# Projections as pairs of 64-row matmuls with max-pass tiles between them, and a written issue order on every engine

## The chip, the core and the metric

The kernel runs on one core of one Trainium2 chip. The metric is the device time of one execution in microseconds. A core has a matrix engine (TensorE, PE in the profile, its weight loads PEld), a vector engine (VectorE, DVE), an activation engine (ScalarE, ACT), a general engine (GpSimd, POOL) and a queue engine that only issues transfers (SyncE, SP).

## The reference

The result mixes two blocks over the same x (2048 tokens, 640 channels) with a gate per token.

```python
x = A_x
g = sigmoid((x * gate_w).sum(-1, keepdims=True))
# A: attention, 32 heads of 20 channels
q, k, v = split(x @ wqkv)
p = softmax(einsum("bhqd,bhkd->bhqk", q, k) * 20 ** -0.5)
a = merge(einsum("bhqk,bhkd->bhqd", p, v)) @ wo
# B: MLP over the token axis
h = layernorm(x, axis=-1, eps=1e-5)
u = gelu(einsum("bsd,sf->bdf", h, w1) + b1)      # f = 1728
b = transpose(einsum("bdf,fs->bds", u, w2) + b2)
return g * a + (1 - g) * b
```

## The kernel before

All matmuls are done on numbers split into a high part in a rounded float32 format and a low part, the rest. A product of two such numbers is three passes: high by high, high by low, low by high (`mm3`, L48). The split is `hi_lo` (L36): ACT copies to the high part, and DVE or POOL subtracts it from the source.

The kernel runs in stages that follow each other on PE.

1. Projections. q and k first: `qk_unit(m, w, q)` (L213) computes 128 channels (m = 0 to 4 are q, 5 to 9 are k) for a quarter q of the tokens, 512 columns. It is 15 full 128-row matmuls into one PSUM bank (five chunks of the 640 input channels by three passes). ACT copies the bank to the high part `evh`, DVE subtracts to the low part `evl`, and SP stores both to DRAM (`q_d`, `k_d`, L223). The units of m = 0 and 5 come first, interleaved, while `load_x` (L229) brings x in by quarters (five loads `xr` of 256 KB each, split into `xh` and `xl`). Then eight units of m = 1 and 6, then 32 v units (L293; 128 tokens by half of the heads, 322 or 320 columns, 15 matmuls each), then the 24 q/k units of the other m. The first v half also yields the sum for the gate and the mean of each token (`gs`); `stats_unit` (L289) runs a Square with accumulation on ACT for the variance. After the v units, `rstd`, `g_t`, `omg` and `b2o` (L319 to L325) are made by a chain that goes back and forth between ACT and DVE. Beside the last 24 units the first half of x is normalised (`h_norm`, POOL) and split (`h_split`, ACT and POOL).
2. The MLP (`mlp`, L489). Its matmuls are pairs of 64-row matmuls into two banks (`pair64`, L43): each uses one half of PE's rows, and the two sums are added when they are read.
3. The attention loop (L672): 16 pairs of heads, 32 iterations each. An iteration makes four score tiles `st` (62 rows by 512 columns), ACT takes their exp into `p`, and PE multiplies `p` by v.
4. The last product with `wo`, and the mix.

The exp needs the maximum of each row of scores beforehand. That is the max pass: a stream of 2048 tiles `s` (60 rows by 512 columns, `s_tiles`, L168), each a matmul and a DVE reduction (`mx`, L180), in pairs of tiles that use the two halves of PE's rows. `s_next` (L155) issues one tile. Each pair of heads p needs a stack in SBUF of its q and k (`load_stack`, 18 loads of 80 and 160 KB, through `base_stack` or, in the loop, `s_stack`). 736 tiles are spread over the MLP (`S_AHEAD`, L538), the other 1312 over the loop. How many an iteration takes is a counter:

```python
due = min((p * 32 + it + 1) * LEFT // (NP * 32 - 28) + 1, LEFT)
take = min(due - given, 3)
```

The PSUM banks are eight: four for `st` (shared with the projections and the MLP), three for `s`, one for the sum of p by v. Tiles with the same tag reuse their buffers in turn, and an instruction waits until the buffer it writes is free.

The order of PE's instructions is written by hand throughout (L32). ACT and DVE join at L236, before the first unit. POOL and SP join only at L328, after the v units; before that a scheduler orders what they issue. The first score stack is issued by POOL (`base_stack(0, False, nc.gpsimd)`, beside the 18th of the last 24 units).

Of the kernel before, what the change touches and what calls it, by code (L numbers as in the profile page):

```python
# [13 lines left out]
P = 128  # L14
S, D, H, DH, F = 2048, 640, 32, 20, 1728
NP = H // 2
NT = S // P
# [11 lines left out]
def gated_mix(ctx, tc, xT, x, wqk, wv0, wv1, wo, w1, w1t, b1, w2, b2, out):  # L29
# [51 lines left out]
    nc.gpsimd.memset(ones_s, 1.0)  # L81
    ones = dram.tile([2, S], F32, name="ones_d")
    nc.gpsimd.dma_start(ones, ones_s)
    eps_t = cp.tile([P, 1], F32, name="eps_t")
# [32 lines left out]
    def base_stack(p, full, eng=nc.sync):  # L117
        ks = k8([P, S], F32R, f"ks{p}_{full}")
        qs = [q4([P, S // 2], F32R, f"qs{p}_{full}_{i}") for i in range(2)]
        load_stack(p, ks, qs, full, eng)  # L120
        return ks, qs
# [74 lines left out]
    xl = [[p1.tile([P, 512], F32R, name=f"xl{c}_{q}") for q in range(4)] for c in range(NC)]  # L196

    def w_dma(m):
# [4 lines left out]
    def load_w(m, raw=None):  # L203
        if raw is None:
            raw = w_dma(m)
        wh = q4([P, NC, P], F32R, f"wh{m}")
        wl = q4([P, NC, P], F32R, f"wl{m}")
        hi_lo(wh, wl, raw, hi_eng=nc.scalar)
        return wh, wl

    accs = iter(range(1000))

    def qk_unit(m, w, q):  # L213
        wh, wl = w
        ps = st_tile([P, 512], f"qk{m}_{q}")
        mm3(ps, [(wh[:, c], wl[:, c], xh[c][q], xl[c][q]) for c in range(NC)])
        hi = p1.tile([P, 512], F32R, tag="evh", bufs=2, name=f"evh{m}_{q}")
        lo = p1.tile([P, 512], F32R, tag="evl", bufs=2, name=f"evl{m}_{q}")
        hi_lo(hi, lo, ps, hi_eng=nc.scalar)
        dst = q_d if m < NC else k_d  # L220
        rows = slice((m % NC) * P, (m % NC + 1) * P)
        cols = slice(q * 512, (q + 1) * 512)
        nc.sync.dma_start(dst[0, rows, cols], hi.bitcast(F32))  # L223
        nc.sync.dma_start(dst[1, rows, cols], lo.bitcast(F32))

# [16 lines left out]
    raws = [w_dma(0), w_dma(NC)]  # L242
    w = {0: load_w(0, raws[0])}
    load_x(0)
    w[NC] = load_w(NC, raws[1])
    for q in range(4):
        if q < 3:
            load_x(q + 1)
        if q == 2:
            w[1] = load_w(1)  # L250
        qk_unit(0, w[0], q)
        qk_unit(NC, w[NC], q)
    pxs.close()
# [14 lines left out]
    def split_wv(half, c):  # L268
        hi_lo(wvs[half][0][c], wvs[half][1][c], wv_raw.pop((half, c)), hi_eng=nc.scalar)

    for c in range(NC):
        load_wv(0, c)
    for n in range(8):
        qk_unit((1, NC + 1)[n // 4], w[(1, NC + 1)[n // 4]], n % 4)
        if n == 0:
            w[NC + 1] = load_w(NC + 1)
        if n >= 3:
            split_wv(0, n - 3)
            load_wv(1, n - 3)
    nc.gpsimd.dma_start(b1_t, b1)  # L280
    nc.gpsimd.dma_start(b2_t, b2)
# [10 lines left out]

    for half in range(2):  # L293
        wvh, wvl = wvs[half]
        width = HALF + 2 if half == 0 else HALF
        for t in range(NT):
# [4 lines left out]
            if n == NT:  # L301
                nc.vector.tensor_scalar_mul(negm, gs[:, :, 1], -1.0 / D)
            if n in (2, 4, 6, 8, 10):
                split_wv(1, n // 2 - 1)
            if n == 2 * NT - 4:
                w[2] = load_w(2)
            ps = st_tile([P, width], f"v{half}_{t}")
            q, cols = t // 4, slice((t % 4) * P, (t % 4 + 1) * P)
            mm3(ps, [(xh[c][q][:, cols], xl[c][q][:, cols], wvh[c], wvl[c]) for c in range(NC)])
            vt = pvp.tile([P, 16, VW], F32, tag="vt", bufs=3, name=f"vt{half}_{t}")  # L310
            nc.gpsimd.memset(vt[:, :, DH], 1.0)
            nc.scalar.activation(vt[:, :, :DH], ps[:, :HALF].rearrange("p (h w) -> p h w", w=DH), AF.Copy)
            nc.sync.dma_start(v_d[half, t], vt.rearrange("p h w -> p (h w)"))
            if half == 0:
                nc.vector.tensor_copy(gs[:, t], ps[:, HALF:])
            else:
                stats_unit(t)
                stats_load(t + 4)
    nc.scalar.activation(rstd, ssq, AF.Sqrt, bias=eps_t, scale=1.0 / D)  # L319
# [4 lines left out]
    nc.vector.tensor_scalar(omg, g_t, -1.0, 1.0, op0=OP.mult, op1=OP.add)  # L324
    nc.vector.tensor_mul(b2o, b2_t, omg)  # L325
    pvs.close()

    ordered.enter_context(tc.manual_schedule(engines={EG.Pool, EG.SP}))  # L328
    hps = ExitStack()
# [33 lines left out]
    AHEAD = 4  # L363
    w_tmp = [k8([P, 16, P], F32R, f"wtmp{i}") for i in range(2)]
    w_raws, w_got = [], []
# [11 lines left out]
    def w_split(k):  # L377
        src, tail = w_list[k]
        raw = w_raws[k]
        n, m = src.shape[1], src.shape[2]  # L380
        if k < AHEAD:
            o = 8 * (k % 2)
            hi, lo = w_tmp[k // 2][:, o: o + 4], w_tmp[k // 2][:, o + 4: o + 8]
# [18 lines left out]
    for n, (m, q) in enumerate(units):  # L402
        if q == 0 and n + 4 < len(units):
            w[units[n + 4][0]] = load_w(units[n + 4][0])
# [8 lines left out]
        if n == 17:  # L413
            w_raw(0)
            w_raw(1)
        qk_unit(m, w[m], q)
        if n in (18, 19):
            w_split(n - 18)
        if n in (20, 21):
            w_raw(n - 18)  # L420
        if n in (22, 23):
            w_split(n - 20)
    p1s.close()

    gps = ExitStack()
    gp = gps.enter_context(tc.tile_pool(name="gp", bufs=1, side="right"))

    soon = []

    def settle(all_=False):  # L430
        for e in soon:
            e[0] -= 1
        due = [e for e in soon if all_ or e[0] <= 0]
        for e in due:
            soon.remove(e)
            e[1]()

# [99 lines left out]

    S_AHEAD = 736  # L538
    STEPS = 2 * ((FT - 1) * 48 + 32 + NT * 40)

    def start_ahead(p):
        if 2 <= p + 1 < 6:
            s_src[p + 1] = base_stack(p + 1, False, None)

    hooks[0] = start_ahead
    steps = mlp(hs)
    done = 0
    for n, _ in enumerate(steps):
        settle()
        while done + 2 <= S_AHEAD and done < S_AHEAD * (n + 1) / STEPS:  # L550
            if done == 48:
                s_src[1] = base_stack(1, False, None)
            if done == 4 * 128 + 40:
# [4 lines left out]
            if drip and done % 4 == 0:  # L558
                drip.pop(0)()
# [26 lines left out]
    M_LAG[0] = 0  # L586
    s_src[6] = s_stack(6)

# [83 lines left out]
    for p in range(NP):  # L672
# [3 lines left out]
        for it in range(32):  # L676
            qh, kt = divmod(it, NT)
            if p + 1 < NP:
                if it == 6:
                    st_src[p + 1] = base_stack(p + 1, True)  # L680
                if it == 12:
                    load_v(p + 1)
                if it == 27:
                    load_m(p + 1, st_src[p + 1][1], 0)
            if it == 11 and p:
                load_m(p, qs, 1)
            if it == 14 and due_stack:
                n = due_stack.pop()
# [109 lines left out]
```

## Time and profile before

| | |
|---|---|
| median of 3 runs | 1846.74 us |
| lowest and highest | 1844.78 and 1847.63 us |
| the profiled execution | 1846.6 us |
| its span, first to last instruction | 1844.8 us |
| granted clock of TensorE over the span | 0.996 |
| q/k units of m = 0, 5, 1, 6 | 7.0 to 65.0 us of the span |
| v units | 65.0 to 136.4 |
| q/k units of the other m | 136.4 to 225.3 |
| MLP | 225.3 to 698.0 |
| attention loop | 698 to 1763 |
| last product and mix | 1763 to 1845 |

The times of the stages are read from the matmuls of PE in the trace, as microseconds from the first instruction. The profiled execution has 1.8 us around its span.

### The profile page before, as it was taken

What the parts mean: (1) busy time and instruction counts of PE and PEld (TensorE: products, weight loads), DVE (VectorE), ACT (ScalarE), POOL (GpSimd) and SP (SyncE); (2) the same over time, 40 slices, a digit from 0 to 9 for tenths busy, and PEclk for the clock granted to TensorE, in tenths of its full rate; (3) what the DMA queues carried; (4) which work ended last, traced back from release to release, by engine and by line L of the source; (5) the groups of instructions that cost most, each with busy time, mean ns of one, the idle gap of its engine ahead of it and who ended that gap; (6) DMA issues with size and microseconds to landing.
All of it is one profiled execution on the core that took longest, in us unless ns stands there. A gap on an engine that the chain in (4) does not pass through costs nothing. (4 is left out here: it accounts for less than half of the span.)

```text
span 1844.8 us, 39129 instructions
## 1 busy us (share of the span) xinstructions
PE 1829.7 (99%) x14978; PEld 1135.2 (62%) x14978; DVE 1428.9 (77%) x2341; ACT 1361.6 (74%) x2688; POOL 637.1 (35%) x900
## 2 busy tenths in 40 slices
PE   9999999999999999999999999999999999999998
PEld 7998799999999994333333333333333333333378
DVE  4202299999999998888888888888888888888137
ACT  4243244465444448999999999999999999999930
POOL 1013478888887770112112111121321211212210
PEclk9999999999999999999999999999999999999999
DMA  8456766566645645504032324213540423301463
GB/s 289 143 169 212 222 173 173 158 194 193 168 139 166 189 136 121 118 15 103 20 85 61 73 42 93 57 50 78 107 103 24 109 47 77 71 14 23 131 219 132
DMA packets 152831, 216.61 MB, mean 117 GB/s; under 512 B 65698, under 2 KB 92082, under 8 KB 148738
## 3 DMA queue, kind: packets, MB, share of 16 engines
q1 hardware_dynamic: 129172, 178.68, 35.4%
q0 software_dynamic: 14688, 20.78, 5.2%
q10 hardware_dynamic: 8784, 14.65, 2.4%
q8 instruction: 118, 1.93, 0.4%
q14 instruction: 69, 0.57, 0.1%
HBM read 165.43 MB, written 48.25 MB: 116 GB/s over the span
## 5 line engine op out<-in xcount | busy, mean ns | idle before, releaser
L180 DVE TENSOR_REDUCE mx<-s 128x1 f32<-128x512 f32 x2048 | 1293.7, 684 | 159.9 <-PE s L178 119.7
L703 ACT ACTIVATE p<-st 128x512 f32<-128x512 f32 x2048 | 1042.1, 615 | 20.9 <-PE s L178 2.2
L700 PEld LDWEIGHTS st<-qs_True,ks_True 62*128 62x128 f32 x2048 | 307.3, 185 | 485.1 <-ACT p L703 312.9
L700 PE MATMUL st<-qs_True,ks_True 62*128 62x512 f32 x2048 | 579.6, 425 | 0.2 <-ACT ty L477 0.2
L637 PE MATMUL pv<-p,v 128*32 128x512 f32 x4096 | 555.5, 605 | 0.2
L178 PE MATMUL s<-sk,sq 60*128 60x512 f32 x1280 | 423.1, 434 | 0.0
L41 POOL TENSOR_TENSOR wl<-wr,wh 128x512 fp32r<-128x512 f32 x228 | 273.6, 1216 | 59.8 <-ACT wh L38 30.9
L624 POOL DMA_DIRECT2D o_d<-oev x128 | 67.0, 524 | 494.3 <-DVE oev L618 491.6
L178 PE MATMUL s<-ks_False,qs_False 60*128 60x512 f32 x768 | 225.1, 397 | 0.4 <-DVE mx L180 0.3
L46 PE MATMUL y<-gh,wh 64*128 64x320 f32 x896 | 216.8, 308 | 0.0
L46 PE MATMUL y<-gl,wh 64*128 64x320 f32 x832 | 210.3, 306 | 0.0
L46 PE MATMUL y<-gh,wl 64*128 64x320 f32 x832 | 209.4, 305 | 0.0
L38 ACT ACTIVATE wh<-wr 128x512 fp32r<-128x512 f32 (+2 forms) x246 | 135.9, 594 | 90.2 <-PE s L178 29.0
L178 PEld LDWEIGHTS s<-sk,sq 60*128 60x128 f32 x1280 | 197.7, 185 | 1.2
L637 PEld LDWEIGHTS pv<-p,v 128*32 128x32 f32 x4096 | 84.9, 108 | 171.4 <-issue 156.4
L46 PE MATMUL u<-hl,wh 64*128 64x320 f32 x864 | 167.1, 306 | 0.0
L46 PE MATMUL u<-hh,wh 64*128 64x320 f32 x864 | 167.1, 306 | 0.0
L46 PE MATMUL u<-hh,wl 64*128 64x320 f32 x800 | 156.9, 306 | 0.4 <-POOL wl L41 0.4
L46 PEld LDWEIGHTS y<-gh,wh 64*128 64x128 f32 x896 | 155.3, 184 | 0.4
L46 PEld LDWEIGHTS y<-gh,wl 64*128 64x128 f32 x832 | 147.0, 184 | 0.3
L46 PEld LDWEIGHTS y<-gl,wh 64*128 64x128 f32 x832 | 146.9, 184 | 0.0
L178 PEld LDWEIGHTS s<-ks_False,qs_False 60*128 60x128 f32 x768 | 124.4, 184 | 1.1 <-DVE mx L180 1.1
(124 smaller groups left out, 1817.6 us busy)
## 6 DMA issues: line engine op xcount, KB each, us to landing
wr<-in_w_dram SPq DMA_DIRECT2D x196, 256.0 KB
ks_True<-k_d SPq DMA_DIRECT2D x96, 160.0 KB
qs_True<-q_d SPq DMA_DIRECT2D x192, 80.0 KB
sk<-k_d SPq DMA_DIRECT2D x60, 160.0 KB
sq<-q_d SPq DMA_DIRECT2D x120, 80.0 KB
v_d<-vt SPq DMA_DIRECT2D x32, 168.0 KB
v<-v_d SPq DMA_DIRECT2D x16, 336.0 KB
xr<-in_xT_dram SPq DMA_DIRECT2D x20, 256.0 KB
```

The lines of the kernel that those rows point to most:

```text
L38: nc.scalar.activation(hi, src, AF.Copy)
L41: (lo_eng or nc.vector).tensor_sub(lo, src, hi.bitcast(F32))
L46: nc.tensor.matmul(ps[k], a[r], b[r], start=start, stop=stop)
L178: nc.tensor.matmul(ps, qs[half][r, t * P:(t + 1) * P], ks[r, kc * 512:(kc + 1) * 512], start=True, stop=True)
L180: nc.vector.tensor_reduce(mx[:, kc, j, t: t + 1], ps, axis=AX.X, op=OP.max)
L624: nc.gpsimd.dma_start(o_d[DH * h: DH * h + DH, cols], ev[r: r + DH, :])
L637: nc.tensor.matmul(pv[r: r + 32, :], v_tiles[p][:, kt, 10 * j: 10 * j + 32], pts[j, c], start=(kt == 0), stop=(kt == NT - 1))
L700: nc.tensor.matmul(ps, ks[r, kt * P:(kt + 1) * P], qs[qh][r, c * 512:(c + 1) * 512], start=True, stop=True)
L703: nc.scalar.activation(pt, ps, AF.Exp, scale=SCALE)
```

## The change

The projections go over to pairs of 64-row matmuls in two banks (`mm_pairs` calls `pair64`). A unit is now read in three steps: ACT copies the first bank at the unit's end, DVE adds the second bank to it three or four PE steps later, and (for q and k) ACT and POOL split it six steps later; SP stores it after twelve. These steps stand in a list `soon`, which `settle` works off at each step of the next unit. v's units are done alike, without the split.

Between the pairs, 176 tiles of the max pass are issued (`Q_S`): four per q/k unit from the fifth unit of m = 1 and 6 on, two per v unit. The MLP keeps its 736 tiles, so 1136 are left to the loop. The score stacks of the first two pairs of heads are loaded in between, one transfer at every second step, by SP. POOL and SP issue in the written order from the start. Subtractions of weights and of q and k go from DVE to POOL; the loads for the statistics go from POOL to SP, and their Square runs two units later. Stacks of the attention loop are asked for at iteration 18 and 23 instead of 6 and 14.

```diff
-        return base.tile(shape, dt, tag="q4", bufs=6, name=name)
+        return base.tile(shape, dt, tag="q4", bufs=4, name=name)
+    Q_S, V_RATE, EVL = 176, 2, 3
...
+    def run(gen, rate):
+        nonlocal done, credit
+        for n, _ in enumerate(gen):
+            settle()
+            if drip and n % 2:
+                drip.pop(0)()
+            credit += rate
+            while credit >= 2 and done < Q_S:
+                credit -= 2
+                s_next()
+                s_next()
+                done += 2
+
+    def mm_pairs(ps, ops):
+        for n, (ah, al, bh, bl) in enumerate(ops):
+            for i, (a, b) in enumerate(((ah, bh), (ah, bl), (al, bh))):
+                pair64(ps, a, b, n == i == 0, n == len(ops) - 1 and i == 2)
+                yield
+
     def qk_unit(m, w, q):
-        ps = st_tile([P, 512], f"qk{m}_{q}")
-        mm3(ps, [(wh[:, c], wl[:, c], xh[c][q], xl[c][q]) for c in range(NC)])
+        ps = [st_tile([P, 512], f"qk{m}_{q}_{i}") for i in range(2)]
+        yield from mm_pairs(ps, [(wh[:, c], wl[:, c], xh[c][q], xl[c][q]) for c in range(NC)])
...
-        hi_lo(hi, lo, ps, hi_eng=nc.scalar)
+        full = lo.bitcast(F32)
+        nc.scalar.activation(full, ps[0], AF.Copy)
+
+        def split():
+            nc.scalar.activation(hi, full, AF.Copy)
+            nc.gpsimd.tensor_sub(lo, full, hi.bitcast(F32))
...
+        soon.append([3, lambda: nc.vector.tensor_add(full, ps[1], full)])
+        soon.append([6, split])
+        soon.append([12, store])
...
-    ordered.enter_context(tc.manual_schedule(engines={EG.Activation, EG.DVE}))
+    ordered.enter_context(tc.manual_schedule(engines={EG.Activation, EG.DVE, EG.Pool, EG.SP}))
...
+        if n == 1:
+            w[NC + 1] = load_w(NC + 1, raws[0])
+            ks = k8([P, S], F32R, "ks0")
+            qq = k8([P, S], F32R, "qs0")
+            s_src[0] = (ks, [qq[:, :S // 2], qq[:, S // 2:]])
+            load_stack(0, *s_src[0], False, None)
+        if n == 4:
+            s_src[1] = base_stack(1, False, None)
+        run(qk_unit((1, NC + 1)[n // 4], w[(1, NC + 1)[n // 4]], n % 4), 4 / 15 if n >= 4 else 0)
...
-            nc.gpsimd.dma_start(xjs[t], x[t * P:(t + 1) * P, :])
+            nc.sync.dma_start(xjs[t], x[t * P:(t + 1) * P, :])
...
+            run(v_unit(half, t), V_RATE / 15)
+            if half and t >= 2:
+                stats_unit(t - 2)
+                stats_load(t + 2)
+    for t in range(NT - 2, NT):
+        stats_unit(t)
     nc.scalar.activation(rstd, ssq, AF.Sqrt, bias=eps_t, scale=1.0 / D)
...
     nc.vector.tensor_mul(b2o, b2_t, omg)
+    settle(True)
     pvs.close()
-    ordered.enter_context(tc.manual_schedule(engines={EG.Pool, EG.SP}))
...
-        if n == 17:
-            s_src[0] = base_stack(0, False, nc.gpsimd)
...
-        qk_unit(m, w[m], q)
+        run(qk_unit(m, w[m], q), 4 / 15)
...
-    S_AHEAD = 736
+    S_AHEAD = Q_S + 736
...
-                if it == 6:
+                if it == 18:
                     st_src[p + 1] = base_stack(p + 1, True)
-                if it == 12:
+                if it == 21:
                     load_v(p + 1)
...
-            if it == 14 and due_stack:
+            if it == 23 and due_stack:
```

More of the change, by code (lines that the diff above doesn't have):

```diff
@@ L118, in base_stack @@
         ks = k8([P, S], F32R, f"ks{p}_{full}")
-        qs = [q4([P, S // 2], F32R, f"qs{p}_{full}_{i}") for i in range(2)]
+        if p % 3 == 1 and not full:
+            qs = [base.tile([P, S // 2], F32R, tag="q4b", bufs=2, name=f"qs{p}_{i}") for i in range(2)]
+        else:
+            qs = [q4([P, S // 2], F32R, f"qs{p}_{full}_{i}") for i in range(2)]
         load_stack(p, ks, qs, full, eng)
@@ L196, in gated_mix, with settle @@
     xl = [[p1.tile([P, 512], F32R, name=f"xl{c}_{q}") for q in range(4)] for c in range(NC)]
+    soon = []
+    def settle(all_=False):
+        for e in soon:
+            e[0] -= 1
+        due = [e for e in soon if all_ or e[0] <= 0]
+        for e in due:
+            soon.remove(e)
+            e[1]()
     def w_dma(m):
@@ L220, in qk_unit @@
[L220 to L224, printed above, removed]
+        lo = p1.tile([P, 512], F32R, tag="evl", bufs=EVL, name=f"evl{m}_{q}")
+        full = lo.bitcast(F32)
[3 more added lines that the diff above has]
+            nc.gpsimd.tensor_sub(lo, full, hi.bitcast(F32))
@@ L226, in gated_mix, with store @@
+        def store():
+            dst = q_d if m < NC else k_d
+            rows = slice((m % NC) * P, (m % NC + 1) * P)
+            cols = slice(q * 512, (q + 1) * 512)
+            nc.sync.dma_start(dst[0, rows, cols], hi.bitcast(F32))
+            nc.sync.dma_start(dst[1, rows, cols], lo.bitcast(F32))
+        soon.append([3, lambda: nc.vector.tensor_add(full, ps[1], full)])
+        soon.append([6, split])
+        soon.append([12, store])
     pxs = ExitStack()
@@ L249, in gated_mix @@
         if q == 2:
[L250 to L252 removed]
+            raws = [w_dma(1)]
+        if q == 3:
+            w[1] = load_w(1, raws[0])
+        run(qk_unit(0, w[0], q), 0)
+        run(qk_unit(NC, w[NC], q), 0)
     pxs.close()
@@ L305, in gated_mix @@
             if n == 2 * NT - 4:
[L306 to L318, printed above, removed]
+                raws = [w_dma(2)]
+            if n == 2 * NT - 2:
+                w[2] = load_w(2, raws[0])
+            run(v_unit(half, t), V_RATE / 15)
[4 more added lines that the diff above has]
+        stats_unit(t)
     nc.scalar.activation(rstd, ssq, AF.Sqrt, bias=eps_t, scale=1.0 / D)
@@ L363, in gated_mix @@
     AHEAD = 4
-    w_tmp = [k8([P, 16, P], F32R, f"wtmp{i}") for i in range(2)]
+    w_tmp = k8([P, 16, P], F32R, "wtmp")
     w_raws, w_got = [], []
@@ L403, in gated_mix @@
         if q == 0 and n + 4 < len(units):
-            w[units[n + 4][0]] = load_w(units[n + 4][0])
-        if n == 17:
-            s_src[0] = base_stack(0, False, nc.gpsimd)
+            raws = [w_dma(units[n + 4][0])]
+        if q == 1 and n + 3 < len(units):
+            w[units[n + 3][0]] = load_w(units[n + 3][0], raws[0])
         if 3 <= n < NT + 3:
@@ L422, in gated_mix @@
             w_split(n - 20)
+    settle(True)
+    while done < Q_S:
+        s_next()
+        done += 1
     p1s.close()
@@ L546, in gated_mix @@
     steps = mlp(hs)
-    done = 0
+    s_src[2] = base_stack(2, False, None)
     for n, _ in enumerate(steps):
         settle()
[L550 to L553, printed above, removed]
+        while done + 2 <= S_AHEAD and done < Q_S + (S_AHEAD - Q_S) * (n + 1) / STEPS:
+            if done == 6 * 128 + 40:
                 st_src[0] = base_stack(0, True, None)
@@ L557, in gated_mix @@
                 drip.append(lambda: load_v(0))
-            if drip and done % 4 == 0:
+            if drip:
                 drip.pop(0)()
```

77 lines of the change are left out of this document (43 added, 34 removed).

## The prediction

> **What bounds the kernel now.** I read the page first, for the share of each engine over the span, then the busy times by stage, then the timeline inside the stages that the change touches. Of the page I need one row, VectorE (DVE) in 40 slices of 46 us.
>
> ```profile
> DVE  4202299999999998888888888888888888888137
> ```
>
> DVE is nearly idle in the first five slices and full after them: that is the room the change wants to use. The busy times by stage (columns: window, total, then PE, PEld, DVE, ACT, POOL busy us with counts, granted clock, DMA share, GB/s):
>
> ```profile
> 7.00:65.00 58.00, 57.55 (x239) 46.26 (x240) 26.30 (x43) 22.39 (x41) 2.26 (x7) 0.97 0.82 269
> 65.00:136.40 71.40, 71.40 (x484) 71.15 (x483) 7.10 (x25) 28.27 (x68) 10.12 (x40) 1.00 0.46 145
> 136.40:225.30 88.90, 85.76 (x361) 68.86 (x360) 20.66 (x33) 29.57 (x56) 37.64 (x54) 0.98 0.72 217
> 225.30:698.00 472.70, 471.89 (x5951) 468.11 (x5952) 465.88 (x760) 226.95 (x461) 382.77 (x394) 1.00 0.58 167
> 698.00:1705.00 1007.00, 1006.66 (x7103) 389.57 (x7100) 851.72 (x1388) 985.63 (x1934) 180.19 (x366) 1.00 0.31 68
> ...
> 213.20:216.60 3.40, 0.33 (x2) 0.00 (x0) 0.67 (x1) 1.66 (x4) 2.66 (x5) 1.00 0.59 131
> 217.20:220.60 3.40, 3.40 (x9) 2.65 (x9) 1.12 (x2) 1.11 (x3) 1.85 (x2) 0.50 1.04 310
> ```
>
> Rows 1 to 3 are the projections, row 4 the MLP, row 5 the attention loop. TensorE is busy throughout, so whatever adds a matmul slot or a stop of PE anywhere adds time, and no later stage gives it back. The last two rows are the one stop of the projections: PE stands 3.4 us and then gets half its clock for 3.4 us, which costs 1.7 us more.
>
> **What an iteration of the loop is worth.** PE in two iterations:
>
> ```profile
> 1000.00 0.49 PE L700 MATMUL st<-qs_True,ks_True 62*128 62x512 f32 x1
> 1000.00 0.72 PE L178 MATMUL s<-sk,sq 60*128 60x512 f32 x2
> ...
> 1000.57 0.40 PE L178 MATMUL s<-sk,sq 60*128 60x512 f32 x1
> ...
> 1002.13 0.49 PE L700 MATMUL st<-qs_True,ks_True 62*128 62x512 f32 x1
> 1002.14 0.72 PE L178 MATMUL s<-sk,sq 60*128 60x512 f32 x2
> ...
> 1004.10 0.49 PE L700 MATMUL st<-qs_True,ks_True 62*128 62x512 f32 x1
> ```
>
> With three max tiles an iteration takes 2.13 us (1000.00 to 1002.13), with two 1.97. The code's counter gives 344 iterations of three and 140 of two: 344 x 2.13 + 140 x 1.97 = 1008.5, and the stage has 1007.0. Near the end, without tiles, ACT sets the pace:
>
> ```profile
> 1711.36 29.11 ACT L703 ACTIVATE p<-st 128x512 f32<-128x512 f32 x59
> ```
>
> Four exps of 29.11 / 59 = 0.49 us are 1.97 us, so two tiles are free and the third costs 0.16. After the change 2048 - 912 = 1136 tiles are left for 484 iterations: 168 with three, 316 with two. **Term 1: 176 x 0.16 = -28 us** (-26 to -30 with the third tile at 0.15 to 0.17).
>
> **What the tiles cost in the projections.** In the MLP the same pairs already stand side by side:
>
> ```profile
> 300.16 0.41 PE L178 MATMUL s<-ks_False,qs_False 60*128 60x512 f32 x2
> 300.39 0.32 PE L46 MATMUL u<-hl,wh 64*128 64x320 f32 x2
> ...
> 301.43 0.41 PE L178 MATMUL s<-ks_False,qs_False 60*128 60x512 f32 x2
> ```
>
> A pair of tiles takes 0.23 us; seven 64-row pairs with 320 columns take 301.43 - 300.39 = 1.04, 0.149 each. A full 128-row matmul of the v projection takes 71.40 / 480 = 0.149, so turning full matmuls into pairs costs nothing at 320 columns, and I take it for 512 too (a tile pair at 512 takes 0.23; a full matmul at most 58.00 / 240 = 0.24). **Term 2: 88 pairs x 0.23 = +20 us.** DVE reads, three per v unit and five per q/k unit, fit under PE there. The MLP keeps its 736 tiles and its time.
>
> **The stop that goes.** The 24 last q/k units take 88.9 us, 24 x 3.5 = 84.0 without stop. Loads of the first score stack sat in POOL's queue, and the normalisation behind them held ACT; they move to SP and earlier. **Term 3: -4.9 us** (0 if another stop takes its place; I take all of it, since POOL issues none of them now).
>
> **What is late next: the head.** SP, ACT, DVE and POOL now issue in written order, and a unit's two banks are freed by an ACT copy and then a DVE add. Call the units A0, B0, A1, B1, A2, B2 (m = 0 and 5, q = 0, 1, 2). Four banks hold two units, no longer four. In the changed order SP has A0's two stores ahead of the third quarter of x (L276); ACT has that quarter's five hi copies ahead of the split of B0; DVE has its five lo subtractions ahead of the add that frees B0's second bank, which B1 writes. In the kernel before, those loads stood at 7.88 and after, before any store:
>
> ```profile
> 7.88 5.36 SPq L232 DMA_DIRECT2D xr<-in_xT_dram  x7
> ...
> 11.60 3.09 DVE L41 TENSOR_TENSOR xl<-xr,xh 128x512 fp32r<-128x512 f32 x5
> 14.61 0.68 DVE L41 TENSOR_TENSOR evl<-qk,evh 128x512 fp32r<-128x512 f32 x1
> ...
> 16.52 0.60 ACT L38 ACTIVATE evh<-qk 128x512 fp32r<-128x512 f32 x1 [2.49 <-PE qk L52]
> ...
> 20.02 0.60 ACT L38 ACTIVATE evh<-qk 128x512 fp32r<-128x512 f32 x1 [0.30 <-PE qk L52]
> ...
> 21.86 1.20 SPq L232 DMA_DIRECT2D xr<-in_xT_dram  x2
> ...
> 26.52 1.26 ACT L38 ACTIVATE xh<-xr 128x512 fp32r<-128x512 f32 x2 [0.84 <-DMA xr<-in_xT_dram]
> ...
> L41 POOL TENSOR_TENSOR wl<-wr,wh 128x512 fp32r<-128x512 f32 x228 | 273.6, 1216 | 59.8 <-ACT wh L38 30.9 <-issue 21.7 <-PE s L178 5.3
> ```
>
> After: A0's add at 14.6 to 15.3 (DVE is held by the five xl before it), split on ACT to 15.9, subtraction on POOL 1.22 to 17.2, its store issued, and only then the five loads, at 17.6 to 19.2. From issue to use a late load took 4.7 us (21.86 to 26.52), so the last is there at about 23.5 (the queue is emptier); hi 0.6, lo 0.7, add 0.7: B0's bank is free at 25.5. PE has ended A1 at 20.0 (the row that waits for PE), so it stands 5.5 us, then loses 1.7 to the clock as above. The same again one quarter later: B0's split and A1's add, split, subtraction and store end at 29.6, loads to 31.2, landed 35.2, bank at 37.2; PE, through B1 at 30.7 and A2 at 34.2, stands 3.0 us, and half of a clock loss (0.8, as 3.0 is a little less than the 3.4 of the row). **Term 4: 5.5 + 1.7 + 3.0 + 0.8 = +11 us**; bounds 7 (loads landing in 2.9, no second clock loss) and 14.
>
> The Trainium skill, "TensorE: Matmul & The Clock Gate", Part 1, says that the gate looks at free-running windows of 3.4 us and halves the clock after a whole idle one. By that page a stop of 5.5 us would be followed by half clock in about 6 of 10 cases and one of 3.0 never: my estimate from it is 1 us for this place, not 2.5. No trace here has enough stops to decide.
>
> **Late at the end of the v projection.** The layer-norm statistics and the gate end in a chain ACT to DVE; before, nothing on PE hung on it.
>
> ```profile
> 133.82 0.82 ACT L291 ACTIVATE xn<-xn,negm 128x640 f32<-128x640 f32 x1
> ...
> 137.93 0.20 ACT L291 ACTIVATION_READ_ACCUMULATOR xn<-xn,negm 128x1 f32 x1
> 138.15 1.28 ACT L319 ACT_TABLE_LOAD   x1
> ...
> 141.06 0.22 ACT L321 ACTIVATE g_t<-gs 128x16 f32<-128x16 f32 x1
> ...
> 142.02 0.18 DVE L325 TENSOR_TENSOR b2o<-b_t,omg 128x16 f32<-128x16 f32 x1
> ```
>
> Now three Squares are left over after the last v unit (0.4 + 3 x 0.82 + 0.2 = 3.1 us on ACT); from the last accumulator read (138.13) to the end of b2o it is 4.07 us; the last v add (about 0.5) and one reduce (0.7) stand behind it on DVE. That reduce is done 8.3 us after v's end, and the fourth max tile needs its bank, three banks being there. PE reaches that tile after nine pairs and a bit, 2.3 us. **Term 5: 6.0 + 1.7 clock = +7.7 us** (5 to 8.5).
>
> **Score stacks beside stores.** Two stacks of 18 loads now go through SP between q/k stores from the second unit of m = 1 on. Alone, 20 such issues took 11.2 us:
>
> ```profile
> 772.88 0.47 SPq L105 DMA_DIRECT2D ks_True<-k_d  x1
> ...
> 784.06 0.27 SPq L115 DMA_DIRECT2D qs_True<-q_d  x1
> ```
>
> The first stack waits for the k store of m = 5 to land, 6 us after that unit; 18 loads at 0.56 and six stores of 256 KB between them at about 0.65 (1.31 / 2, the spacing of late loads above) need 14 us, 3 to 4.7 to land: there at 23 to 25, or 19 if loads and stores overlap. The first tile stands 16.8 us after it (four units of 3.5 and twelve pairs). **Term 6: +6.5 us** with its clock loss, from the middle (bounds 0 and 10).
>
> **The start of the MLP.** Its weight loads stand behind the last store:
>
> ```profile
> 227.29 0.38 SPq L224 DMA_DIRECT2D k_d<-evl  x1
> 230.72 3.67 SPq L374 DMA_DIRECT2D wr<-in_w_dram  x8
> ...
> 236.04 0.41 PE L46 MATMUL u<-hh,wl 64*128 64x320 f32 x2 [0.39 <-POOL wl L41]
> ```
>
> PE already waits there. The last store now comes after copy, add, split and POOL's 1.22 instead of split and subtraction, 1.5 to 2 us later. **Term 7: +1.5 us** (0 to 3).
>
> **Covered.** In the loop, stacks are asked for at iteration 18 and 23 instead of 6 and 14; the SP rows above run as soon as buffers free, so I cost this at nothing; uncovered, a stack of 11 us against the 9 iterations left could cost 2 us once or twice. MLP drips come twice as often, under PE.
>
> **Sum** against the profiled execution of 1846.6 us (span 1844.8; median of the runs 1846.74): -28 + 20 - 4.9 + 11 + 7.7 + 6.5 + 1.5 = +13.8, so 1860 us.
>
> **Rivals.** (A) Only the head stops: terms 5 and 6 are hidden because DVE and SP catch up in time: -0.4 us, 1846. For it: PE's banks and buffers allow a unit or two of slack; against: the waits are single-file on DVE. Chance 0.15. (B) Faster: the two-tile iterations leave PE enough slack to take the third tile for nothing in a mix of two to one, so that all run at ACT's 1.97: 168 x 0.16 = 27 us less, 1833. It decides if three-tile iterations after two-tile ones take under 2.05. Against it: now they take 2.13 between twos as well. Chance 0.08. (C) SP does not catch up after the first stack: the second stack's 11 us delay stores, split and banks of the units after: up to 12 more, 1872. Chance 0.12. (D) The change does not do what it says: 64-row pairs with 512 columns do not run side by side, and 600 more slots of 0.23 come on top: about 2000. The 0.23 tile pair speaks against it. Chance 0.02. My forecast: 0.63.
>
> About 0.2%, 3.7 us, is what a measurement can tell from no change. Slower: forecast, C, D and 0.02 of A, 0.79; same 0.07 and faster 0.14 from A and B. The range 1848 to 1873 takes in the forecast's bounds and C and leaves out B, D and half of A.
>
> **Where to look.** Right: PE stops near 20, 34, at the first max tile, and 2 us into the first q/k unit after v, each ending with DVE or a DMA, with half clock behind the long ones; the loop shorter by 26 to 30 us; no stop near the old 213. Wrong: if PE stops less than 12 us in all before the MLP, or if an iteration of three tiles falls under 2.05.

## The result: slower by 1.7%, more than twice what was forecast

The changed kernel takes 1878.2 us (median of 4 runs, 1873.4 to 1879.4), the kernel before, run beside it, 1846.4; the ratio is 1.0173, with an interval of 1.0161 to 1.0185. The sign was right. The forecast was 1860 and its range ended at 1873: the loss is 32 us where 14 were expected. The profiled execution has a span of 1877.6 us against 1844.8, and the difference of 32.8 us is split up below.

First, the stages of the kernel after (window, total, then PE, PEld, DVE, ACT, POOL busy us with counts, granted clock, DMA share, GB/s): 16 q/k units (m = 0, 5, 1, 6), v, 24 q/k units, MLP, loop, output.

```profile
7.00:95.50 88.50, 66.82 (x494) 56.29 (x496) 33.02 (x51) 33.01 (x57) 24.88 (x21) 0.85 0.64 192
95.50:177.20 81.70, 81.26 (x1027) 79.50 (x1023) 55.78 (x115) 28.98 (x82) 13.63 (x45) 1.00 0.50 160
177.20:280.30 103.10, 97.48 (x822) 80.34 (x820) 77.01 (x127) 44.71 (x81) 65.51 (x68) 0.97 0.54 169
280.30:760.50 480.20, 475.36 (x5956) 471.46 (x5954) 467.22 (x763) 228.18 (x462) 385.53 (x399) 0.99 0.62 169
760.50:1793.60 1033.10, 1032.52 (x7282) 387.46 (x7278) 754.82 (x1215) 1022.99 (x2050) 190.66 (x372) 1.00 0.32 68
1793.60:1877.60 84.00, 75.92 (x481) 73.16 (x480) 48.86 (x84) 8.76 (x10) 7.36 (x13) 0.96 0.56 192
```

The same view of the kernel before, for the two stages that the prediction did not show whole:

```profile
698.00:1763.50 1065.50, 1065.04 (x7461) 407.03 (x7458) 859.21 (x1397) 1043.04 (x2050) 193.15 (x383) 1.00 0.31 70
1763.50:1844.80 81.30, 73.59 (x481) 70.55 (x480) 48.73 (x84) 8.75 (x10) 7.33 (x13) 0.98 0.58 199
```

The loop gave back what it should and more: 1033.1 instead of 1065.5. All the rest became longer: the first 16 units by 30.5 (88.5 against 58.0), v by 10.3, the last 24 units by 14.2, the MLP by 7.5, the output by 2.7. In the first row PE is busy for 66.8 of 88.5 us, at 0.85 of its clock, where it used to be busy throughout.

Whom PE waits for up to 300 us is told by the table of waits of the kernel after (us in total, times, longest; its three longest rows):

```profile
PE qk L46 <- DVE evl L266: 12.4, 2, 8.6
PE s L180 <- DMA qs<-q_d: 8.5, 1, 8.5
PE s L180 <- DVE mx L182: 7.3, 2, 5.6
```

Four of these stops lie ahead of the MLP. Two in the head (8.6 us, up to 28.0, and 3.8 us, up to 41.6) wait for the add that frees a bank. One (8.5, up to 79.1) stands at the first max tile, and one (5.6, up to 185.4) 2 us into the first q/k unit after v. (The other wait of the last row, 1.7 us, is at the start of the MLP.) That is where the prediction had put them; their sizes and one cause are not as it said. A pair of stops in the MLP, between 526.4 and 529.5, was not forecast at all:

```profile
PE u L46 <- ACT wh L38: 1.4, 1, 1.4
PE u L46 <- POOL wl L41: 1.1, 1, 1.1
```

And each stop has a second price. The windows right behind the five places, with one from the middle of the second stop (37.1) and one that holds most of the fifth (525.2):

```profile
28.00:33.70 5.70, 5.68 (x26) 4.44 (x28) 0.69 (x1) 1.75 (x3) 2.57 (x2) 0.50 0.53 191
37.10:40.50 3.40, 0.68 (x6) 0.22 (x4) 2.22 (x4) 2.52 (x4) 0.00 (x0) 1.00 0.44 169
41.60:47.30 5.70, 5.67 (x26) 4.44 (x28) 0.69 (x1) 1.75 (x3) 2.56 (x2) 0.50 0.61 211
79.10:84.90 5.80, 5.76 (x28) 4.92 (x30) 2.41 (x4) 0.96 (x2) 0.88 (x1) 0.50 0.78 183
185.40:190.70 5.30, 5.28 (x24) 4.17 (x26) 2.73 (x5) 1.22 (x2) 0.16 (x1) 0.50 0.22 63
525.20:528.60 3.40, 1.84 (x20) 1.23 (x16) 2.42 (x4) 2.63 (x5) 1.25 (x2) 1.00 0.78 202
528.60:535.40 6.80, 5.91 (x42) 5.72 (x44) 2.58 (x4) 2.95 (x6) 6.40 (x6) 0.50 0.44 113
```

Behind each stop PE works for 5.3 to 5.9 us at half clock, so it loses 2.6 to 3.0 us more. In the trace of before it was 3.4 us and 1.7, and that is the price the prediction used.

### The profile page after: what moved, and what is told of

Its sections match the earlier page's. It is cut to its first block, busy times and chain, and to the rows that moved or that the text cites. A ratio compares the mean times of both kernels' runs of the same rounds, so it can differ in the third digit from the quotient of the medians.

```text
span 1877.6 us, 41814 instructions
## 1 busy us (share of the span) xinstructions
PE 1834.0 (98%) x16058; PEld 1151.4 (61%) x16058; DVE 1437.5 (77%) x2355; ACT 1369.0 (73%) x2744; POOL 691.4 (37%) x924
## 5 line engine op out<-in xcount | busy, mean ns | idle before, releaser
L767 ACT ACTIVATE p<-st 128x512 f32<-128x512 f32 x2048 | 1022.1, 626 | 8.8 <-PE s L180 0.7
L764 PEld LDWEIGHTS st<-qs_True,ks_True 62*128 62x128 f32 x2048 | 278.8, 185 | 472.3 <-issue 285.0
L764 PE MATMUL st<-qs_True,ks_True 62*128 62x512 f32 x2048 | 548.1, 428 | 0.3 <-ACT ty L543 0.2
L180 PE MATMUL s<-sk,sq 60*128 60x512 f32 x1024 | 355.8, 450 | 0.0
L41 POOL TENSOR_TENSOR wl<-wr,wh 128x512 fp32r<-128x512 f32 (+1 forms) x235 | 285.4, 1229 | 88.3 <-ACT wh L38 50.8
L38 ACT ACTIVATE wh<-wr 128x256 fp32r<-128x256 f32 (+2 forms) x245 | 135.7, 594 | 77.9 <-PE s L180 34.3
L701 PEld LDWEIGHTS pv<-p,v 128*32 128x32 f32 x4096 | 84.9, 108 | 171.0 <-issue 157.2
L180 PEld LDWEIGHTS s<-sk,sq 60*128 60x128 f32 x1024 | 155.7, 184 | 1.4 <-ACT p L767 0.5
L180 PE MATMUL s<-ks_False,qs_False 60*128 60x512 f32 x512 | 153.6, 393 | 0.0
L46 PE MATMUL qk<-xh,wh 64*128 64x512 f32 x360 | 112.0, 413 | 13.6 <-DVE evl L266 12.4
```

Of the source, the lines that this page charges most:

```text
L38: nc.scalar.activation(hi, src, AF.Copy)
L41: (lo_eng or nc.vector).tensor_sub(lo, src, hi.bitcast(F32))
L46: nc.tensor.matmul(ps[k], a[r], b[r], start=start, stop=stop)
L180: nc.tensor.matmul(ps, qs[half][r, t * P:(t + 1) * P], ks[r, kc * 512:(kc + 1) * 512], start=True, stop=True)
L701: nc.tensor.matmul(pv[r: r + 32, :], v_tiles[p][:, kt, 10 * j: 10 * j + 32], pts[j, c], start=(kt == 0), stop=(kt == NT - 1))
L764: nc.tensor.matmul(ps, ks[r, kt * P:(kt + 1) * P], qs[qh][r, c * 512:(c + 1) * 512], start=True, stop=True)
```

## The experiments

Ten kernels were run. Each is the changed kernel with the edit shown, except where it says otherwise.

**Loads of x ahead of the stores (e1).**

```diff
+        if q == 0:
+            x_dma(1)
         if q < 3:
-            load_x(q + 1)
+            x_split(q + 1)
+        if q < 2:
+            x_dma(q + 2)
```

Here `x_dma` issues the five loads of a quarter and `x_split` makes their high and low parts.

> Only the loads of the third and fourth quarter of x are issued on SP ahead of the first stores; ACT and DVE keep their order. Theory Q (SP's single file: the loads behind A0's and A1's stores come late, and all else follows from that): both stops of the head (8.6 us up to 28.0, 3.8 us up to 41.6) and their half-clock stretches go, the eight units of m = 0 and 5 end near 36.5 us instead of 54, and the time falls by 16 to 18, to 1860 us. Rival A (the adds are the cause, behind five subtractions on DVE): the subtractions still stand ahead of them, so B1 still stops for a few us and the time stays above 1868. Rival D (the DMA engines cannot bring x and take the stores in that time): the loads still land late, half of the stop stays, 1868 to 1872.

(By the code, the loads of the third quarter stand ahead of all stores, those of the fourth behind the two stores of the first unit, ahead of the rest.)

Measured: 1863.4 us, ratio to before 1.0080 (1.0065 to 1.0096), where the change has 1.0173. The waits of PE up to 50 us:

```profile
PE qk L46 <- DVE evl L266: 2.6, 2, 1.3
PE qk L46 <- ACT xh L38: 1.1, 1, 1.1
```

12.4 us of waiting for the add have become 2.6, though the add still stands behind five subtractions on DVE. The v projection begins at 80.3 us instead of 95.5. Late loads were the cause, not DVE's order, and the DMA engines can carry them.

**Adds ahead of the subtractions (e2).**

```diff
-        soon.append([3, lambda: nc.vector.tensor_add(full, ps[1], full)])
+        add = lambda: nc.vector.tensor_add(full, ps[1], full)
+        if m in (0, NC):
+            add()
+        else:
+            soon.append([3, add])
```

> Only the adds of the units of m = 0 and 5 are issued on DVE at the end of their own unit, ahead of the next quarter's subtractions; the loads stay behind the stores. Theory Q: PE gets through B1 to 22.5 us, and then stops at A2 for the quarter that lands at 24 to 26; the second stop still ends near 40 with the quarter behind A1's stores; the time falls by 0 to 3, to 1875 us. Rival A (the adds are the cause): both stops go, 1860 us.

Measured: 1874.1 us, ratio 1.0139 (1.0118 to 1.0160): 4 us less than the change. The longest of PE's waits up to 60 us:

```profile
PE qk L46 <- ACT evl L253: 6.3, 2, 4.1
```

The add no longer holds PE; now ACT's copy does, since the hi copies of the late quarter stand ahead of it. The stops are half as long (6.3 us for 12.4) and go by another name: one queue was cured, and the same late loads came through the next. With e1 this settles the head.

**The projections without SP's and POOL's written order (e10).** This undoes one of the three parts of the change.

```diff
-    ordered.enter_context(tc.manual_schedule(engines={EG.Activation, EG.DVE, EG.Pool, EG.SP}))
+    ordered.enter_context(tc.manual_schedule(engines={EG.Activation, EG.DVE}))
...
     pvs.close()
+    ordered.enter_context(tc.manual_schedule(engines={EG.Pool, EG.SP}))
```

> Pairs, tiles and stacks as in the change, but SP and POOL are issued in written order only from the end of the projections on, as in the kernel before: in the projections the scheduler places them, and in the built program it puts all loads of x ahead of the stores, and most transfers of the first stack's first q half ahead of those of k. Theory: the head's part of the loss came from the written order of SP alone, so both head stops go as they do with the loads moved by hand (1863 us); the k rows of the stack still come between the stores, so most of the stop ahead of the first tile stays: 1858 to 1863 us. Rival (POOL's subtractions, in written order behind the weights', hold the stores): the same, or slower than 1866, since the scheduler's order of POOL is as full.

Measured: 1867.3 us, ratio 1.0120 (1.0101 to 1.0139), 4 us above what was expected, and by its time alone within what the rival allowed. The waits of PE up to 300 us decide between the two:

```profile
PE s L180 <- DMA qs<-q_d: 11.5, 1, 11.5
...
PE qk L46 <- DVE evl L266: 3.2, 2, 1.9
```

The head is as good as with the loads moved by hand (all but two of x's loads stand ahead of the first store). The stop at the first max tile grew from 8.5 to 11.5 us; in the built order four loads of x rows for the statistics, 320 KB each, now stand ahead of the first stack's k rows, which may be why. So the written order cost the head. The stack's stop comes in the scheduler's order too, where the stack's loads stand between the stores as well. The 4 us lie elsewhere: the loop takes 1037.6 us in this run, where the change has 1033.1, with a stop near 1522 and half clock behind it. PE's wait from 744 to 1781 us:

```profile
PE st L765 <- DMA qs_True<-m_d: 2.8, 1, 2.8
```

The loop's code is that of the change, so its later stacks, which the prediction put at nothing, can be late there; in the change's own trace they were not.

**No max tiles in the units of m = 6 (e4).** 160 tiles in place of 176; all loads stay where they are.

```diff
-    Q_S, V_RATE, EVL = 176, 2, 3
+    Q_S, V_RATE, EVL = 160, 2, 3
...
-        run(qk_unit(...), 4 / 15 if n >= 4 else 0)
+        run(qk_unit(...), 0)
```

> No max tiles in the four units of m = 6; 160 tiles ahead of the MLP instead of 176, 16 more in the loop; loads and stores as before. Theory: the stop of 8.5 us up to 79.1 and the half clock behind it (2.9 lost) go, 8 tile pairs less save 1.8 there, 16 more third tiles cost 16 x 0.2 = 3.2 in the loop: 1877.6 - 8.5 - 2.9 - 1.8 + 3.2 = 1867.6 us. Rival (the stack's loads hold the stores on SP and the DMA engines, and by them splits and banks, so PE stops whether a tile asks for the stack or not): a stop of 4 us or more stays between 66 and 85 us, 1872 us or more.

Measured: 1892.4 us, ratio 1.0246: slower by 14 us than the change. That has a cause of the experiment's own. 160 + 736 = 896 is 7 x 128, so the tiles of the eighth pair of heads start inside the loop, and the code that opens them there asks for the next stack a second time (54 transfers of `sk` where the change has 48). The transfers of the m rows queue behind it on SP, and PE stands for 14.0 us near 940. Row of the page, and the wait between 800 and 1000 us, both of e4:

```profile
sk<-k_d SPq DMA_DIRECT2D x54, 160.0 KB
```

```profile
PE s L180 <- DMA qs_True<-m_d: 14.0, 1, 14.0
```

What the run was made for can be read ahead of that. The three longest waits of PE from 44 to 100 us, and the window (columns as above):

```profile
PE v L46 <- ACT wv L38: 3.8, 1, 3.8
PE qk L46 <- ACT evl L253: 1.8, 1, 1.8
PE v L46 <- ACT evl L253: 1.3, 1, 1.3
```

```profile
62.00:94.00 32.00, 23.56 (x190) 19.24 (x187) 4.15 (x6) 8.89 (x17) 11.87 (x11) 0.97 0.78 231
```

Without a tile that asks for the stack, PE still stands 6.9 us in these three, which end at 92.7, 75.9 and 86.1 us, and has half clock behind the longest (91.9 to 98.8). The last v unit ends 1.9 us sooner than in the change (175.3 for 177.2), about what the eight tile pairs cost that are no longer there, so nothing of the stop is regained. What ACT waits for from 60 to 96 us:

```profile
ACT evh L256 <- DMA q_d<-evh: 15.2, 4, 4.7
...
ACT evh L256 <- DMA k_d<-evh: 7.1, 2, 4.6
```

A split needs the buffer of a store that has not landed; six times ACT stands up to 4.7 us for it, and the copies that free banks and the v weights' splits queue behind. The sign that the rival was given, one stop of 4 us or more between 66 and 85 us, did not come; its substance, that PE stops with the tile or without it, holds. Term 6's reading (the first tile arrives before its stack) names where PE stood, and not all of why.

**Both stacks loaded during v (e9).** 176 tiles as before, but no stack load and no tile in the units of m = 1 and 6; three transfers per v unit instead (`drip_step`: one transfer at every fifth step), the first stack from the first v unit on and the second from the tenth.

```diff
-            load_stack(0, *s_src[0], False, None)
-        if n == 4:
-            s_src[1] = base_stack(1, False, None)
...
+            if n == 0:
+                drip_step[0] = 5
...
+                load_stack(0, *s_src[0], False, None)
+            if n == 9:
+                s_src[1] = base_stack(1, False, None)
-            run(v_unit(half, t), V_RATE / 15)
+            run(v_unit(half, t), 80 / 24 / 15 if n >= 8 else 0)
```

> 176 tiles ahead as in the change, but no stack is loaded and no tile stands in the units of m = 1 and 6: the first stack is loaded three transfers per v unit from the first v unit on, the second from the tenth, and the 80 tiles that stood there and in v stand in the v units from the ninth on. Theory B (traffic: two stacks of 1.9 MB beside eight units' stores of 4 MB and 1.6 MB of v weights are more than the DMA engines carry in that stretch): the stop of 8.5 us and the late v start both go, v begins at about 84 us, and the time falls by 10 to 11, to 1867 us. Rival (the stores are late by SP's written order alone, whatever is between them): v units stop in the same way while the stacks load, 3 us or less gained, 1875 us or more.

Measured: 1861.4 us, ratio 1.0082 (1.0067 to 1.0098). Between 44 and 170 us, up to the stop behind v, all waits of PE together are

```profile
PE v L46 <- DVE vt L359: 0.2, 1, 0.2
```

and v begins at 81.3 us instead of 95.5. The same stacks on the same queue cost PE no wait where their neighbours are v's stores. One stack is 6 transfers of 160 KB and 12 of 80, 1.9 MB. In the change two of them fell on 28 us (eight units of 3.5), with 4.2 MB of stores and 1.6 MB of v weights: 9.6 MB, which would be 340 GB/s. The window of e4 carried 231 GB/s at a share of 0.78, and the busiest rows of the kernel before 269 over 58 us and 310 over 3.4 us. So there were more bytes than any window shown here carried. But SP's single file has a part in it as well. In the change, one ACT row and three of SP:

```profile
63.55 0.63 ACT L256 ACTIVATE evh<-evl 128x512 fp32r<-128x512 f32 x1 [1.17 <-DVE evl L266]
65.38 3.02 SPq L98 DMA_DIRECT2D qs<-q_d  x4
68.98 1.24 SPq L98 DMA_DIRECT2D ks<-k_d  x3
70.69 0.34 SPq L263 DMA_DIRECT2D q_d<-evh  x1
```

The high part of the second unit of m = 1 is ready at 64.2 and its store is issued at 70.69, behind seven transfers of the stack. e9 changes the neighbours, the pace of the loads and the place of the tiles at once, so it shows a cure; how much is the DMA engines' capacity, how much the file, and whether more than two buffers for `evh` would have hidden it, was not tried apart.

The gain in time, 17 us, is more than this place: the stop behind v is shorter too (3.8 us and one window of half clock, where the change has 5.6 and two), and the last 24 units take 100.2 us instead of 103.1.

**The gate's chain on DVE later (e3).**

```diff
-    nc.vector.reciprocal(rstd, rstd)
...
-    nc.vector.tensor_mul(b2o, b2_t, omg)
...
+        if n == 1:
+            gate_chain()
```

`gate_chain` holds the five DVE instructions, `n == 1` is the second q/k unit after v.

> Only the five DVE instructions that finish the layer norm's scale and the gate (reciprocal to b2o) are issued after the second q/k unit that follows v instead of ahead of the last v add. Theory: the stop of 5.6 us up to 185.4 goes and with it the half clock up to 190.7 (5.3 us, 2.7 lost); the last 24 q/k units take 94.8 instead of 103.1 and the time falls by 8, to 1869 us. Rival (ACT, with three squares and two table loads, holds the first copy of the unit just as long): the stop moves two units on and at most 3 us are gained, 1875 us.

Measured: 1870.1 us, ratio 1.0114 (1.0097 to 1.0131). The last 24 units and PE's waits from 160 us to 300:

```profile
176.10:272.40 96.30, 95.25 (x823) 88.67 (x821) 77.73 (x127) 44.56 (x81) 65.47 (x68) 1.00 0.57 181
```

```profile
PE s L180 <- DVE mx L182: 2.7, 2, 1.7
```

96.3 us instead of 103.1, at full clock. Five small DVE instructions that waited for ACT were worth 7 us by their place alone.

**The stop filled with idle work (e8).**

```diff
+            if i == 7:
+                for j in range(24):
+                    nc.tensor.matmul(idle, xh[0][0][:, :P], xh[0][0], start=(j == 0), stop=(j == 23))
```

> 24 matmuls on data that nobody uses stand in the place of the stop in the first q/k unit after v (about 5.6 us of work where PE stood 5.6 us); nothing else is changed, so the wait is there but PE is not idle in it. Theory G (the 5.3 us of half clock behind the stop cost 2.7 us over and above it): the stretch stays at full clock, the last 24 q/k units take 100.4 instead of 103.1 us, 1875 us. Rival (the units behind the stop are held by their copies on ACT anyway, so the clock costs nothing): 1877 to 1878 us.

Measured: 1874.0 us (1868.0 to 1878.6), ratio 1.0148 (1.0128 to 1.0168): too wide by itself, but the stage says it.

```profile
176.10:276.90 100.80, 100.80 (x847) 83.57 (x846) 76.95 (x127) 44.70 (x81) 65.57 (x68) 1.00 0.55 173
```

DVE is as late as before, PE is never idle in the wait, the clock stays at 1.00, and the 24 units take 100.8 instead of 103.1. The half clock behind a 5.6 us stop is worth 2.3 us of its own here, where nothing later waits longer in exchange.

**Stack loads paused round the start of the MLP's second half (e5).**

```diff
+    PAUSE = (STEPS // 2 - 64, STEPS // 2 + 32)
...
-            if drip:
+            if drip and not PAUSE[0] <= n < PAUSE[1]:
                 drip.pop(0)()
```

`drip` is the list of stack loads that are issued one at a time between PE's steps.

> Only the stack loads that are issued between the MLP's steps are held back from 64 steps ahead of the start of its second half to 32 steps after it. Theory: the two stops of 1.4 and 1.1 us near 527 and their two windows of half clock go, the MLP takes 475 instead of 480.2 us; 1872 us. Rival (the loads of x at the start of the second half are late for another reason, buffers or the weights' loads): both stops stay.

Measured, one run: 1870.4 us. The MLP:

```profile
278.00:753.30 475.30, 472.64 (x5958) 468.97 (x5955) 467.42 (x763) 227.89 (x462) 385.13 (x399) 1.00 0.63 170
```

475.3 instead of 480.2, and no wait of PE at that place. The span is 9.0 us shorter than that of after; the other 4 lie in the first 16 units (86.0 for 88.3) and the output (82.3 for 84.0), where this run has the code of the change.

**All four cures (e6).** The edits of e1, e3, e5 and e9 in one kernel.

> Four edits at once: loads of x ahead of the stores, stacks and tiles in v from the ninth unit on, the DVE chain of the gate two units later, drips paused round the start of the MLP's second half. Theory (each of the stops is paid for by its own queue and they add up): 1877.6 less 15 (head), 11 (stacks), 7.5 (chain), 5 (drips) = 1839 us, faster than the kernel before by 0.4%. Rival (what is saved in one place is waited for in the next, since DMA traffic and not order is the limit from the head to the MLP): 1848 us or more.

Measured: 1839.1 us (1837.9 to 1841.3, 5 runs) against 1845.9; ratio 0.9962, interval 0.9950 to 0.9975. This beats both kernels, the one before by 0.4%. Its first four stages:

```profile
7.00:67.80 60.80, 57.51 (x481) 46.27 (x483) 23.83 (x37) 32.03 (x57) 25.90 (x21) 0.97 0.68 229
67.80:151.30 83.50, 82.99 (x1044) 81.12 (x1042) 63.45 (x129) 29.12 (x83) 13.10 (x45) 1.00 0.65 195
151.30:246.10 94.80, 94.77 (x817) 80.16 (x816) 77.19 (x127) 44.67 (x81) 65.36 (x67) 1.00 0.57 182
246.10:719.80 473.70, 471.91 (x5956) 469.35 (x5954) 466.96 (x763) 227.92 (x462) 385.11 (x399) 1.00 0.62 171
```

The projections take 60.8 + 83.5 + 94.8 = 239.1 us where the change had 273.3 and the kernel before 218.3. What is left over before, 20.8 us, is the price of 88 tile pairs and some small stops, less the gain of the old stop; the loop returns 32.6. By medians the single gains are 15, 17, 8 and 8 us, 48 in all, and together they give 39. The single gains hold more than their own stop: e9's has 3 us of the stop behind v, which e3 cures too, and e3 and e5 have 2 us each in the first 16 units, which they did not touch. The sum made from the stops themselves, 38.5, came within 1 us of the time's 39 and 3 of the span's 41.5.

**The kernel before once more (b0).**

> The kernel before, profiled once more, for its last stage: 81.3 us from the first output matmul to the end in the first profile, 83.9 in the kernel after it. If the difference belongs to the change, this profile has 81 to 82 us again; if it is the spread of one execution, it lies between 81 and 84.5, as the stages of the other kernels do.

Measured: 1846.5 us; the last stage, from 1763.0 to 1844.6, has 81.6 us.

## Why the prediction was right or wrong

Where the forecast failed: the head (term 4) and the first stack (term 6) were sized too small, a tile pair in v costs 0.32 us and not 0.23 (term 2), and the stack loads inside the MLP, put at nothing, cost 5.5. Term by term:

- **What bounds the kernel.** Right: time went where PE stopped or got slots more. No later stage gave a stop back.
- **Term 1 (loop, -28).** Mechanism right, size 32.4. The timeline of the loop of after, PE's first score matmul of five iterations, with the third tile of the one that has it:

```profile
1001.45 0.50 PE L764 MATMUL st<-qs_True,ks_True 62*128 62x512 f32 x1
...
1003.35 0.49 PE L764 MATMUL st<-qs_True,ks_True 62*128 62x512 f32 x1
...
1003.92 0.39 PE L180 MATMUL s<-sk,sq 60*128 60x512 f32 x1
...
1005.51 0.49 PE L764 MATMUL st<-qs_True,ks_True 62*128 62x512 f32 x1
...
1007.40 0.49 PE L764 MATMUL st<-qs_True,ks_True 62*128 62x512 f32 x1
...
1009.33 0.50 PE L764 MATMUL st<-qs_True,ks_True 62*128 62x512 f32 x1
```

  Two tiles: 1.90, 1.89, 1.93 us; three: 2.16. These few rows overstate it: 168 x 2.16 + 316 x 1.91 = 966 would be 42 us less than the 1008.5 of before. Counted over all iterations that have tiles, by the starts of their exps in the trace, two tiles take 1.95 us on average (1.98 before) and three 2.14 (2.13 before). So an iteration of two among others of two is a little shorter, and a tile moved away is worth 32.4 / 176 = 0.184 us instead of 0.16. Rival B asked for threes under 2.05; that did not come.
- **Term 2 (88 pairs, +20).** Right that pairs of 64 rows cost what full matmuls cost: in e6's first 16 units, without tiles, PE is busy for 57.51 us, before for 57.55 (they last 60.8 against 58.0 by small stops), and four v units take 8.93 us before and, as pairs without tiles, in e9 (90.6 to 99.5). A tile pair costs 0.225 in a q/k unit ((94.8 - 84.0) / 48) as read, but 10.3 / 32 = 0.32 in a v unit (0.30 by e6: 12.1 / 40). With 8 pairs in the units of m = 6 that is about 23. The MLP's price did not carry over to v, and no run shows why.
- **Term 3 (-4.9).** Right; PE has no stop near the old place, and e6's 24 units hold 84.0 plus 48 pairs.
- **Term 4 (head, +11).** Places and mechanism right (e1, e2, e10), size 8.6 + 3.8 of stops and 2.8 + 2.9 of clock, 18 (v began 15.2 us earlier in e1, which still has 3.7 us of stops there). Two steps failed. The estimate added one hi, one lo and one add behind the last load. The rows say that four of the quarter's five loads were there together, and their four copies stood in line (ACT, then DVE, of after), so that the bank came free at 28.0 and not at 25.5:

```profile
24.02 2.62 ACT L38 ACTIVATE xh<-xr 128x512 fp32r<-128x512 f32 x4 [1.60 <-DMA xr<-in_xT_dram]
```

```profile
24.68 2.69 DVE L41 TENSOR_TENSOR xl<-xr,xh 128x512 fp32r<-128x512 f32 x4 [1.54 <-ACT xh L38]
27.28 0.68 DVE L266 TENSOR_TENSOR evl<-qk,evl 128x512 f32<-128x512 f32 x1
```

  And the clock was priced from one stop as 1.7 and 0.8, where it cost 2.8 and 2.9. Part of that is the chance of one execution. e3, e4, e5, e8 and e9 have the same head, and by their waits and clock it cost 14 to 17 us there. In e5 the second stop, 4.7 us, was followed by one window of half clock, 1.7 us lost:

```profile
41.20:44.60 3.40, 3.40 (x18) 2.63 (x18) 0.69 (x1) 1.54 (x3) 2.19 (x2) 0.50 0.47 174
```

  The estimate that the prediction drew from the Trainium skill, "TensorE: Matmul & The Clock Gate", Part 1 (1 us here) was further off still.
- **Term 5 (end of v, +7.7).** Right: 5.6 + 2.6 = 8.2, and e3 shows the cause.
- **Term 6 (first stack, +6.5).** The stop is there, 8.5 + 2.9 = 11.4, beyond the bound of 10. The stack came as late as the upper reading said: 24.5 us after the last unit of m = 5 (54.6 to 79.1), where 23 to 25 was estimated for loads one behind the other. The first tile stands behind eight pairs of its unit, not twelve, so PE was there after 16.0 us (70.6) and not 16.8. The step that failed is the choice of the middle between this and overlapped loads, with a clock loss of 1.7. The reading of the cause was wrong in part: e4 shows that PE stops without the tile, and e9 that the same stacks cost no wait in v. Too many bytes in one stretch and SP's single file both have a part, and their shares are open. Rival C had this in part, and its 1872 was the nearest of all.
- **Term 7 and what was covered.** The start of the MLP cost its 1.5, but not by the wait that was named: PE stands 1.7 us for a max reduction, which DVE does only behind the last unit's add, and 0.6 for the weights, where before it stood 0.3 and 0.4. That the stack loads inside the MLP cost nothing failed: moved by 176 tiles, a stack's 18 loads fell on the change from the first half to the second, where SP also fetches x. The two short stops and the half clock behind them are 2.5 + 3.0 us; e5 shows it.
- **The output, +2.7.** Not forecast. The code is the same, and PE is busy 2.3 us longer in it (75.9 for 73.6). The half clock behind the second of two stops there (3.9 us together, 2.6 before) is enough for it:

```profile
1822.30:1829.10 6.80, 6.11 (x22) 5.94 (x23) 3.90 (x7) 0.00 (x0) 0.00 (x0) 0.50 0.81 262
```

  In the first profile of before the clock is 1.00 until PE has ended. Two profiles of the kernel before have 81.3 and 81.6 us, after and its variants 81.0 to 84.4, mostly over 83; a reload of the sums lands about 1 us later there. Why it does, and so why the stops are longer, is open.

By rows: -32.4 + 23 - 4.9 + 18 + 8.2 + 11.4 + 7.5 + 2.7 = +33.5, against 32.8 measured. Of the 19 to 20 us that the forecast missed, 7 were in the head, 5 in the stack, 6 in the MLP, 3 in v and 3 in the output; the loop returned 4 more. The 18 of term 4 and the 2.7 of the output are those of the profiled execution, the slowest of the four.

## What to carry to other kernels

Writing the order of a DMA queue by hand means writing where every load stands, not only the ones in mind: a store ahead of a load passes its own wait on to all that the load feeds. Price a stop of PE as its length plus the half clock behind it, and look for the half clock's end in the trace rather than taking it from one stop. When work is moved earlier, move its loads by a count of the bytes in each stretch and of what will stand behind them in their queue, and look at every boundary that the shifted schedule now meets.

## What the runs showed of the hardware

Half clock begins and ends on a grid of 3.41 us. Its ends at 33.7, 47.3, 84.9, 190.7 and 535.4 lie 4, 11, 31 and 101 steps apart; stops are not on that grid, so two like stops can differ in price: the second stop of the head, 3.8 us, had two windows of half clock behind it in the change, and 4.7 us had one in e5 (41.2 to 44.6). That is the free-running window of the Trainium skill, "TensorE: Matmul & The Clock Gate", Part 1. The page's condition, a whole idle window, is not what the rows show. From 37.1 to 40.5 PE was busy for 0.68 us, from 525.2 to 528.6 even for 1.84 of 3.4, and both times the next two windows were half. Stops of 1.3 us in e1 and e6 left the clock alone. About half a window idle was enough here, and a window at half clock in which PE came back after 1.1 us (41.6, in the one that began at 40.5) was followed by another.

The price of two max tiles depends on their neighbours: 0.23 us among matmuls of 512 columns and in the MLP, 0.30 to 0.32 in v. The loads of weights are busy for 79.5 of 81.7 us in v, but for 471.5 of 480.2 in the MLP as well, so they alone do not tell the two apart; what does was not tried.
